# List-scheduling all engine streams of a cosine-attention + projection kernel from one dependency graph, with an early first projection

## Chip, cores, metric

The kernel runs on one core of a Trainium2 chip. The metric is the device time of one execution in microseconds (us), as the median of several. The profiled execution has its own length, called the span. Nearly all executions were in the fast state; one each of tp_late, skd_r3 and best_u3 was slow, and a few of the kernel before. The medians in the tables are over all executions; for these three the text uses those of the fast ones. Chips and calls differ by about 0.7% (the kernel before had medians from 539.53 to 543.15 us), so each run is compared with executions of the kernel before on the same chip in the same call.

## The reference, cut to what matters

```python
q_n = q / (norm(q) + 1e-6);  k_n = k / (norm(k) + 1e-6)   # 8 batches, 12 heads, 448 tokens, 64 wide
attn = softmax(q_n @ k_n.T / 0.1);  o = attn @ v
x = o.transpose(0, 2, 1, 3).reshape(3584, 768)
h = x @ w_in               # 768 x 2048: the first projection
out = (h * cos(h)) @ w_out # 2048 x 768: the second projection
```

## The kernel before

Heads are worked in pairs: 48 pairs, three to a unit, two units (six pairs) to a batch. A pair is transposed, scored, exponentiated on ACT and attended on PE, which also forms the row sums of the exponentials. Six pairs of a batch make `xT`, the input of the batch's first projection: 96 matmuls of 128x448, in eight groups each followed by a sine on ACT and a multiply on DVE. The second projection is 896 matmuls in all, 16 per half tile, and is dealt out in eights between the parts of later pairs, to fill PE while ACT works.

Each engine runs its own stream in the order in which the program adds operations. Waits come from keys: an operation waits for the last writer of what it reads, and for the last writer and all readers of what it writes.

```python
for t in reads:
    w = self.writer.get(t)
    if w is not None: dep(w, True)
for t in writes:
    w = self.writer.get(t)
    if w is not None and w is not o: dep(w, False)
    for r in self.readers.get(t, ()): dep(r, False)      # write after read
...
self.ops[eng].append(o)                                  # program order is engine order
```

The row sums lie in a layout in which a reciprocal is slow. So each unit sends them on a round trip: gathered by four DMAs to 128 partitions, inverted on DVE, written to DRAM, read back broadcast, then multiplied.

```python
def around(u, kq):
    ...
    if u >= 1:
        if kq == 2: gather(u - 1)                        # SP: sums <- xu
        if kq == 5: recip(u - 1); spread(u - 1)          # DVE; SP: scr <- rcp
        if kq == 8: broadcast(u - 1)                     # SP: RB <- scr
    if u >= 2 and kq < UP: normalise(u - 2, kq)          # DVE: xT <- xu * RB
LAG = 4
for u in range(NU):
    for p in range(UP):
        ...                                              # scores, attend, transposes, fills
        if p == 0 and u >= LAG and u % 2 == 0:
            m1((u - LAG) // 2)                           # first projection of batch 0 in unit 4
```

Because of `LAG = 4`, the first projection of batch 0 comes after 13 pairs. Until then there is nothing to fill PE with.

Of the kernel before, what the change touches and what calls it, by code (L numbers as in the profile page):

```python
# [13 lines left out]
class Op:  # L14
    __slots__ = ("eng", "fn", "pos", "waits", "inc", "count", "dma", "dcount", "known")


class Program:
# [4 lines left out]

    ENGINES = ("PE", "ACT", "DVE", "POOL", "SP")

    def __init__(self, new_sem):
        self.new_sem = new_sem
        self.ops = {e: [] for e in self.ENGINES}
        self.known = {e: {} for e in self.ENGINES}
        self.writer = {}  # L30
        self.readers = {}
        self.dma_count = {}
        self.by_dma = {}

    def op(self, eng, fn, reads=(), writes=(), dma=None):
        o = Op()
        o.eng, o.fn, o.dma, o.inc, o.count = eng, fn, dma, False, None
        o.pos = len(self.ops[eng])
        need = {}

        def dep(y, raw):
            if y.dma is not None:
                k, v = ("dma", y.dma), y.dcount
            else:
                if y.eng == eng and (dma is None and (not raw or eng == "PE")):
                    return
                k, v = ("eng", y.eng), y.pos + 1
            if k not in need or need[k][0] < v:
                need[k] = (v, y)

        for t in reads:
            w = self.writer.get(t)
            if w is not None:
                dep(w, True)
        for t in writes:
            w = self.writer.get(t)
            if w is not None and w is not o:
                dep(w, False)
            for r in self.readers.get(t, ()):
                dep(r, False)  # L60
        known = self.known[eng]
        o.waits = []
        for k, (v, y) in sorted(need.items(), key=lambda i: str(i[0])):
            if known.get(k, 0) >= v:
                continue
            o.waits.append((k, v, y))
            if y.dma is None:
                y.inc = True
        for k, v, y in o.waits:
            known[k] = max(known.get(k, 0), v)  # L70
            for kk, vv in y.known.items():
                if known.get(kk, 0) < vv:
                    known[kk] = vv
        o.known = dict(known)
        if dma is not None:
            self.dma_count[dma] = self.dma_count.get(dma, 0) + 1
            o.dcount = self.dma_count[dma]
        for t in writes:
            self.writer[t] = o
            self.readers[t] = []  # L80
        for t in reads:
            self.readers.setdefault(t, []).append(o)
        self.ops[eng].append(o)
        return o

    def final_dma(self, names):
        o = Op()
        o.eng, o.dma, o.inc, o.count, o.known = "SP", None, False, None, {}
        o.fn, o.pos = None, len(self.ops["SP"])
        o.waits = [(("dma", n), self.dma_count[n], None) for n in names]  # L90
        self.ops["SP"].append(o)

    def emit(self, nc):
        sems = {}
        for e in self.ENGINES:
            n = 0
            for o in self.ops[e]:
                if o.inc:
                    n += 1
                    o.count = n  # L100
            if n:
                sems[("eng", e)] = self.new_sem()
        for d in self.dma_count:
            sems[("dma", d)] = self.new_sem()

        def run(name, e):
            for o in self.ops[name]:
                for k, v, y in o.waits:
                    e.wait_ge(sems[k], 16 * v if k[0] == "dma" else y.count)
                if o.fn is None:  # L110
                    continue
                inst = o.fn(e)
                if o.dma is not None:
                    inst.then_inc(sems[("dma", o.dma)], 16)
                elif o.inc:
                    inst.then_inc(sems[("eng", name)], 1)
# [24 lines left out]
def bass_cosine_attention__then__act_gcu_kernel(  # L141
# [15 lines left out]
    NG = UP * NU  # L157
    NJ = 4
# [31 lines left out]
    vraw = sb("vraw", [NP, UH * NJ * D], F32)  # L190
# [9 lines left out]
    RB = sb("RB", [128, UP * S], F32)  # L200
# [5 lines left out]
    ones = sb("ones", [NP, 32], BF16)  # L206
# [19 lines left out]
    RBv = RB.ap().rearrange("p (g s) -> p g s", g=UP)  # L226
# [3 lines left out]
    PHs = [("AV", AVv), ("SC0", SCv[0]), ("SC1", SCv[1])]  # L230

    P = Program(new_sem)


    P.op("POOL", lambda e: e.iota(iot.ap(), [[1, NP]], base=0, channel_multiplier=-1), writes=["iot"])
    P.op("DVE", lambda e: e.tensor_scalar(ident.ap(), iot.ap(), 0, None, ALU.is_equal), ["iot"], ["ident"])
    P.op("DVE", lambda e: e.memset(cst.ap()[:, 0:1], math.pi / 2.0), writes=["cst"])
    P.op("DVE", lambda e: e.memset(cst.ap()[:, 1:2], 1e-12), writes=["cst"])
    P.op("POOL", lambda e: e.memset(ones.ap(), 1.0), writes=["ones"])
    P.op("ACT", lambda e: e.preload_act_table_set("natural_log_exp_and_others"))  # L240


# [4 lines left out]
    def load(u, p0, p1):  # L247
        i = u % 2
        keys = [("raw", i, p) for p in range(p0, p1)]
        h = slice(2 * p0, 2 * p1)  # L250
        for x, t in enumerate((q, k)):
            o = P.op("SP", lambda e, x=x, t=t: e.dma_start(
                rawv[i][:, h, NJ * x : NJ * x + NJ, :].rearrange("p h s d -> p h (s d)"),
                src(t, u, 2 * p0, 2 * (p1 - p0))), writes=keys if x == 0 else [], dma="raw%d_%d" % (i, p0))
        for t in keys:
            P.writer[t] = o

    def load_v(u):
        P.op("SP", lambda e: e.dma_start(vraw.ap().rearrange("p (h c) -> p h c", h=UH), src(v, u, 0, UH)),
             writes=["vraw"], dma="vraw")  # L260


    def squares(u, p, eng="POOL"):
        i = u % 2
        x = raw[i].ap()[:, p * 2 * NS * D : (p + 1) * 2 * NS * D]
        if eng == "ACT":
            P.op("ACT", lambda e: e.activation(sq[p].ap(), x, ACT.Square), [("raw", i, p)], [("sq", p)])  # L267
        else:
            P.op(eng, lambda e: e.tensor_tensor(sq[p].ap(), x, x, ALU.mult), [("raw", i, p)], [("sq", p)])  # L269

    def reduce(u, p):
        i = u % 2
        P.op("DVE", lambda e: e.tensor_reduce(out=n2[i].ap()[:, p * 2 * NS : (p + 1) * 2 * NS],  # L273
                                              in_=sq[p].ap().rearrange("p (x d) -> p x d", d=D),
                                              axis=mybir.AxisListType.X, op=ALU.add),
             [("sq", p)], [("n2", i, p)])

    def rnorm(u, p0, p1):
        i = u % 2
        w = slice(p0 * 2 * NS, p1 * 2 * NS)  # L280
        P.op("ACT", lambda e: e.activation(lnn[i].ap()[:, w], n2[i].ap()[:, w], ACT.Ln, bias=cst.ap()[0:NP, 1:2]),
             [("n2", i, p) for p in range(p0, p1)] + ["cst"], [("lnn", i, p0)])
        P.op("ACT", lambda e: e.activation(rn[i].ap()[:, w], lnn[i].ap()[:, w], ACT.Exp, scale=-0.5),  # L283
             [("lnn", i, p0)], [("rn", i, p) for p in range(p0, p1)])

    def scale(u, p, parts=(("POOL", 0, 8),)):
        i = u % 2
        h = slice(2 * p, 2 * p + 2)
        for eng, s0, s1 in parts:
            P.op(eng, lambda e, s0=s0, s1=s1: e.tensor_tensor(  # L290
                qksv[i][:, s0:s1, h, :].rearrange("p s h d -> p h s d"), rawv[i][:, h, s0:s1, :],
                bass.AP(rn[i], p * 2 * NS + s0, [[UH * NS, NP], [NS, 2], [1, s1 - s0], [0, D]]), ALU.mult),
                [("raw", i, p), ("rn", i, p)], [("qks", i, p, s) for s in range(s0, s1)])

    def vcast(u, p):
        i = u % 2
        w = slice(2 * NJ * D * p, 2 * NJ * D * (p + 1))
        P.op("POOL", lambda e: e.tensor_copy(va[i].ap()[:, w], vraw.ap()[:, w]), ["vraw"], [("va", i, p)])


    def transposes(g):
        u, p, j = g // UP, g % UP, g % 2
        i = u % 2
        for s in range(NS):
            P.op("PE", lambda e, s=s: e.transpose(TP.ap()[:, NP * s : NP * s + NP],  # L305
                                                  qksv[i][:, s, 2 * p : 2 * p + 2, :], ident.ap()),
                 [("qks", i, p, s), "ident"], ["TP"])
        P.op("DVE", lambda e: e.tensor_copy(qkT[j].ap(), TP.ap()[:, 0 : 2 * S]), ["TP"], [("qkT", j)])  # L308

    def scores(g, c):  # L310
        j, z = g % 2, c % 2
        for a in range(2):
            r = slice(64 * a, 64 * a + 64)
            P.op("PE", lambda e, r=r, a=a: e.matmul(  # L314
                SCv[z][0:NP, a, 0:S], qkT[j].ap()[r, S + NP * c : S + NP * c + NP], qkT[j].ap()[r, 0:S],
                start=True, stop=True), [("qkT", j)], ["SC%d" % z])
        P.op("ACT", lambda e: e.activation(PXv[j][:, c], SCv[z][0:NP, :, 0:S], ACT.Exp, scale=1.0 / TAU),  # L317
             ["SC%d" % z], [("PX", j, c)])

    def attend(g, eng):  # L320
        u, p, j = g // UP, g % UP, g % 2
        i = u % 2
        for c in range(NJ):
            for a in range(2):
                P.op("PE", lambda e, a=a, c=c: e.matmul(  # L325
# [268 lines left out]
```

## Time and profile before

| | before |
|---|---|
| median (range, 3 runs) | 539.53 us (539.48 to 541.54) |
| span | 538.9 us |
| PE busy | 471.6 us, 88% |
| ACT, DVE, POOL busy | 288.4, 257.7, 220.5 us |

The first fence shows stretches of the kernel before (the windows view): start and end, length, busy time of each engine with its instruction count, mean granted clock of TensorE, DMA share of its 16 engines, GB/s.

```profile
0.00:118.00 118.00, 72.71 (x444) 27.92 (x445) 51.95 (x63) 53.87 (x73) 80.89 (x73) 0.90 0.88 188
166.73:279.20 112.47, 110.19 (x803) 55.61 (x802) 63.89 (x75) 74.80 (x89) 52.94 (x37) 1.00 0.49 125
444.00:538.90 94.90, 82.10 (x456) 44.46 (x456) 29.78 (x40) 17.92 (x18) 0.00 (x0) 0.98 0.17 45
```

A cycle of two batches in the middle has PE busy for 110.2 of 112.5 us at full clock: order alone cannot gain much there. The beginning loses 45 us and the end 13.

The second fence is a part of the chain of waits of the kernel before, the work that ended last followed back: start, length, what.

```profile
83.86 8.01 DMA RB<-scr
...
96.43 7.60 DMA sums<-xu
...
106.91 5.17 DMA RB<-scr
...
112.11 0.46 DVE xT L371
...
118.02 1.11 PE AV L381 x5
```

Most of this part of the chain is the round trip: gather 7.6 us, broadcast 5 to 8. The third fence is the timeline of PE in the kernel before: start, length, instructions, and in brackets the idle time before them with its releaser.

```profile
110.08 2.43 PE L381 MATMUL AV<-xT,W 128*128 128x448 bf16 x12
112.35 4.70 PE L381 MATMUL SC<-xT,W 128*128 128x448 bf16 x24
118.02 2.43 PE L381 MATMUL AV<-xT,W 128*128 128x448 bf16 x12 [0.97 <-DVE gT L386]
```

The first projection really begins at 110.08. The entry at 118.02 in the chain is where the chain comes back to PE after a small stop inside the projection.

### The profile page before, as it was taken

To read this page: it belongs to the slowest core of one execution; us is meant where nothing else is said; L and a number is where in the kernel's file an instruction comes from. 1 tells how busy PE (TensorE), PEld (TensorE's weight loads), DVE (VectorE), ACT (ScalarE), POOL (GpSimd) and SP (SyncE) were. 2 spreads that over 40 slices of the span, in tenths; PEclk is the share of its full clock that TensorE was granted. 3 is DMA by queue.
4 is the path that set the end of the run, shared out by engine and by line. 5 is a ranking of instruction groups with operands and counts; after the bars stand their busy time and mean duration, and the time that the engine had idled before them with its cause. 6 is when DMAs were issued, how large, how long until landed. Compare 5 with 4: busy or idle time off the path is not lost.

```text
span 538.9 us, 7716 instructions
## 1 busy us (share of the span) xinstructions
PE 471.6 (88%) x3200; PEld 230.7 (43%) x3200; DVE 257.7 (48%) x311; ACT 288.4 (54%) x344; POOL 220.5 (41%) x169
## 2 busy tenths in 40 slices
PE   1477674798999999999999999999899999779896
PEld 0122221243444545455445554554455445344463
DVE  3415553554366546544755465556475324413421
ACT  2355353565777586647774777367756674202200
POOL 4796956530855085505580459018721400000000
PEclk9999976799999999999999999999999999899999
DMA  8699899680467056902781287217501331210023
GB/s 202 125 204 210 162 201 198 152 203 1 112 174 189 1 127 170 235 1 59 210 211 26 60 209 190 75 30 205 145 24 31 85 82 24 60 58 1 29 60 88
DMA packets 51490, 62.36 MB, mean 116 GB/s; under 512 B 9984, under 2 KB 44288, under 8 KB 51456
## 3 DMA queue, kind: packets, MB, share of 16 engines
q1 hardware_dynamic: 47552, 55.58, 40.7%
q0 software_dynamic: 3904, 6.29, 7.1%
q8 instruction: 25, 0.41, 0.3%
q14 instruction: 9, 0.07, 0.0%
HBM read 56.62 MB, written 11.18 MB: 126 GB/s over the span
## 4 chain that ended last, share of the span: by engine, by line
PE 64%; DMA 16%; DVE 10%; ACT 4%; SPq 3%; POOL 2%; issue 1%; DVEq 0%; ACTq 0%
PE PO L420 20%; PE SC L381 16%; PE AV L381 10%; DMA sums<-xu 6%; DMA RB<-scr 6%; PE AV L325 5%; PE SC L314 5%; PE AV L331 3%; DMA raw<-in_k_dram 3%; DVE xT L371 3%; ACT PX L317 3%; PE SC L420 2%; DVE n L273 2%; PE TP L305 2%; SPq L345 2%; DMA scr<-rcp 2%
## 5 line engine op out<-in xcount | busy, mean ns | idle before, releaser
L317 ACT ACTIVATE PX<-SC 112x896 bf16<-112x896 f32 x192 | 164.0, 915 | 85.8 <-PE SC L314 85.8
L290 POOL TENSOR_TENSOR qks<-raw,rn 112x1024 bf16<-112x1024 f32 (+1 forms) x48 | 90.5, 1884 | 193.1 <-ACT rn L283 193.0
L420 PE MATMUL PO<-W,gT 128*128 128x384 bf16 x784 | 143.1, 330 | 9.5 <-DVE osb L428 9.5
L420 PEld LDWEIGHTS PO<-W,gT 128*128 128x128 bf16 x784 | 71.5, 98 | 78.9 <-issue 18.3
L314 PE MATMUL SC<-qkT 64*112 64x448 bf16 x384 | 70.4, 428 | 32.6 <-ACT PX L317 16.7
L269 POOL TENSOR_TENSOR sq<-raw 112x1024 bf16<-112x1024 f32 x47 | 92.2, 1985 | 9.0 <-DMA raw<-in_k_dram 8.9
L381 PE MATMUL SC<-xT,W 128*128 128x448 bf16 x480 | 94.7, 352 | 0.0
L384 ACT ACTIVATE cosb<-SC,cst 128x896 f32<-128x896 f32 x40 | 40.3, 1008 | 49.9 <-PE SC L381 47.8
L371 DVE TENSOR_TENSOR xT<-xu,RB 128x448 bf16<-128x448 f32 x48 | 47.3, 995 | 38.6 <-DMA RB<-scr 38.6
L381 PEld LDWEIGHTS SC<-xT,W 128*128 128x128 bf16 x480 | 47.0, 98 | 43.8
L386 DVE TENSOR_TENSOR gT<-SC,cosb 128x896 bf16<-128x896 f32 x40 | 43.6, 1090 | 40.8 <-ACT cosb L384 40.7
L273 DVE TENSOR_REDUCE n<-sq 112x16 f32<-112x1024 bf16 x48 | 57.5, 1209 | 7.7 <-ACT sq L267 4.1
L381 PE MATMUL AV<-xT,W 128*128 128x448 bf16 x288 | 58.4, 353 | 2.1 <-ACT xu L335 1.0
L325 PE MATMUL AV<-PX,va 112*64 112x448 bf16 x384 | 54.5, 414 | 0.0
L308 DVE COPY qkT<-TP 128x896 bf16<-128x896 bf16 x48 | 29.7, 618 | 51.4 <-PE TP L305 51.4
L428 DVE COPY osb<-PO 128x384 f32<-128x384 f32 x49 | 27.0, 551 | 54.1 <-PE PO L420 53.9
L384 ACT ACTIVATE cosb<-AV,cst 128x896 f32<-128x896 f32 x24 | 24.2, 1008 | 52.8 <-PE AV L381 51.5
L314 PEld LDWEIGHTS SC<-qkT 64*112 64x112 bf16 x384 | 21.8, 136 | 66.8 <-ACT PX L317 34.7
L305 PE MATMUL TP<-ident,qks 112*128 112x112 bf16 x384 | 31.8, 235 | 18.8 <-POOL qks L290 10.8
L381 PEld LDWEIGHTS AV<-xT,W 128*128 128x128 bf16 x288 | 27.7, 98 | 29.4 <-issue 2.9
L386 DVE TENSOR_TENSOR gT<-AV,cosb 128x896 bf16<-128x896 f32 x24 | 26.1, 1089 | 29.1 <-ACT cosb L384 29.1
L305 PEld LDWEIGHTS TP<-ident,qks 112*128 112x128 bf16 x384 | 26.1, 109 | 32.7 <-POOL qks L290 14.7
(32 smaller groups left out, 230.5 us busy)
## 6 DMA issues: line engine op xcount, KB each, us to landing
vraw<-in_v_dram SPq DMA_DIRECT2D x16, 672.0 KB, 6.0
RB<-scr SPq DMA_DIRECT2D x32, 336.0 KB, 4.7
raw<-in_q_dram SPq DMA_DIRECT2D x15, 672.0 KB, 7.9
raw<-in_k_dram SPq DMA_DIRECT2D x15, 672.0 KB, 9.4
W<-in_moe_w_in_dram POOLq DMA_DIRECT2D x12, 256.0 KB, 6.5
W<-in_moe_w_out_dram POOLq DMA_DIRECT2D x8, 384.0 KB, 8.9
out_dram<-osb SPq DMA_DIRECT2D x8, 336.0 KB, 3.2
out_dram<-osb SPq DMA_DIRECT2D x8, 288.0 KB, 2.6
```

The costliest lines, as they stand in the source:

```text
L269: P.op(eng, lambda e: e.tensor_tensor(sq[p].ap(), x, x, ALU.mult), [("raw", i, p)], [("sq", p)])
L273: P.op("DVE", lambda e: e.tensor_reduce(out=n2[i].ap()[:, p * 2 * NS : (p + 1) * 2 * NS], in_=sq[p].ap().rearrange("p (x d) -> p x d", d=D ...
L290: P.op(eng, lambda e, s0=s0, s1=s1: e.tensor_tensor(qksv[i][:, s0:s1, h, :].rearrange("p s h d -> p h s d"), rawv[i][:, h, s0:s1, :], bass ...
L305: P.op("PE", lambda e, s=s: e.transpose(TP.ap()[:, NP * s : NP * s + NP], qksv[i][:, s, 2 * p : 2 * p + 2, :], ident.ap()), [("qks", i, p, ...
L314: P.op("PE", lambda e, r=r, a=a: e.matmul(SCv[z][0:NP, a, 0:S], qkT[j].ap()[r, S + NP * c : S + NP * c + NP], qkT[j].ap()[r, 0:S], start=T ...
L317: P.op("ACT", lambda e: e.activation(PXv[j][:, c], SCv[z][0:NP, :, 0:S], ACT.Exp, scale=1.0 / TAU), ["SC%d" % z], [("PX", j, c)])
L325: P.op("PE", lambda e, a=a, c=c: e.matmul(AVv[64 * a : 64 * a + 64, 0, 0:S], vav[i][:, NJ * (2 * p + a) + c, :], PXv[j][:, c, a, :], start ...
L371: P.op("DVE", lambda e: e.tensor_tensor(xTv[b % 2][:, UP * i + p, :], xuv[i][:, 0, p, :], RBv[:, p, :], ALU.mult), ["RB", ("xu", i, p)], [ ...
L381: P.op("PE", lambda e, n=n, c=c, a=a: e.matmul(ph[:, a, 0:S], W1v[:, c, 128 * n : 128 * n + 128], xTv[b % 2][:, c, :], start=(c == 0), sto ...
L384: P.op("ACT", lambda e: e.activation(cosv[cz], ph[:, :, 0:S], ACT.Sin, bias=cst.ap()[:, 0:1], scale=1.0), [name, "cst"], [("cos", cz)])
L386: P.op("DVE", lambda e: e.tensor_tensor(gTv[:, 2 * gi : 2 * gi + 2, S * (b % 2) : S * (b % 2) + S], ph[:, :, 0:S], cosv[cz], ALU.mult), [n ...
L420: P.op("PE", lambda e, po=po, f=f, col=col, hf=hf: e.matmul(po[:, 0:HW], gTv[:, f, col : col + 128], W2v[:, f, HW * hf : HW * hf + HW], st ...
```

## The change

Operations are now collected with costs and dependencies, and every engine's stream is list-scheduled from one model, `play`. The first projection of batch 0 follows pairs 0 to 5 directly; their sums are inverted on the spot (logarithm and exponential on ACT, or a reciprocal on DVE) without the round trip. Later ones come after pair 3 of the batch after next. The second projection is spread evenly over pairs, matmuls on zeros fill early gaps of PE, normalising moves to POOL, loads of units 2 and later move from SP to ACT, weights come in 4 + 4 large DMAs instead of 20, score weights are 128 wide, `RB` is doubled, and the last second projections use several PSUM banks.

```diff
+    RATE = {"SP": 220e3, "ACT": 220e3, "POOL": 220e3}          # bytes per us
+    def play(self):
+        ...
+        server = {e: 0.0 for e in self.RATE}
+            if o.dma is not None:
+                o.end = max(o.end + 1.7, o.start + 2.2)
+                if o.nbytes > self.SMALL:
+                    server[e] = max(server[e], o.start + 1.0) + o.nbytes / self.RATE[e]
+                    o.end = max(o.end, server[e] + 1.0)
... (an engine takes the ready operation with the earliest deadline; the result is a fixed stream)
+    load_v(0, [("raw", 0, 0)])
+    load_v(1, [("raw", 0, 0)])
+    for x in range(NQ):
+        load_w1(x, [("raw", 0, 1)])
...
+    DIRECT = {0: "ACT", 1: "DVE", 2: "ACT", 3: "DVE", 4: "ACT", 5: "ACT"}
...
+    for g in range(PB):
+        pair(g, 0, 0)
+    load(2, 0, UP, reads=[("W1", 1)])
+    norms(2, 0)
+    for x in range(NQ):
+        load_w2(x, [("W1", 1)])
+    load(3, 0, UP, reads=[("W2", 0)])
+    attend(PB - 1, DIRECT[PB - 1])
+    load_v(3)
+    transposes(PB)
+    m1(0)
... (pairs 6 to 47; from b = 2 on, the first projection of batch b - 1 after pair 3 of batch b)
+    attend(NG - 1, None)
+    chain(NU - 1)                                              # the round trip of the last unit
+    banks[0] = [("PO", PO.ap())] + [(n, x[:, 0, :]) for n, x in PHs[1:]]
+    m2_fill(10 ** 6)
+    m1(B - 1)
```

The `reads` of loads have no data in them. They only say "not before this has landed". So that `load_v` and `load_w1` come after the first q/k loads, they are entered as readers of `raw` buffer 0.

## The prediction

> **What bounds the kernel now.** PE is busy 471.6 of 538.9 us (88%, page). By windows: 72.7 of the first 118 us; then 110.2 of 112.5 us in each cycle of two batches, clock 1.00; the last 95 us lose 12 again. So the steady state is bound by TensorE and the loss is the beginning: up to 118 us the chain of waits is mostly the row-sum round trip (gather, reciprocal, spread, broadcast). The first of eight first projections starts at 118.0 us, after 13 of 48 head pairs; nothing else can fill TensorE before it. The granted clock is 0.60 from 75 to 100 us.
>
> **What must be done anyway (timeline, chain).** First projection: 96 matmuls in 18.16 us, 145 us in all. Second: 16 in 2.60 us, 146 us in all. Attention on TensorE: about 3.0 us a pair (scores twice 0.52 to 0.62, attend 0.88, sums 0.49, transposes 0.49), some 0.1 of each being the change of mode. That matches the Trainium skill, "TensorEngine Tiling (Array Packing)", Key Properties (changing the tiling mode drains the array): eight second-projection matmuls take 1.41 us after such a change, 1.30 without.
>
> **What changes.**
> 1. Batch 0 is projected directly behind its six pairs, whose sums are inverted on ACT or DVE without the round trip. First exponential at about 10.5 us, from 12.7. Then ACT has 24 exponentials of 0.84 us, squares, eight half-width Ln/Exp and small ones, about 30 us, so attention ends near 42. But in the instruction order 45 filler matmuls and the transposes of pair 6 stand ahead of the projection; those wait for unit 2, whose load waits for a part of W1, then 6 us of POOL squares and a scale. I expect the projection at about 49 us (44 to 55).
> 2. 42 pairs, not 35, then come behind that point: +21 us.
> 3. Fillers keep the clock up early and compute nothing.
> 4. Steady state: the same matmuls. 128-wide score weights and order save some 0.1 us a pair; normalising moves from DVE to POOL (about 0.9 us each, estimated from POOL's 1.9 us for 1024 columns). A batch cycle of 54 to 56 us, from 56.2.
> 5. Pairs 6 to 15 have little filling: ACT and PE both need about 4.3 us a pair; 4 to 6 us are lost to coupling.
> 6. End: three banks end the single-bank waits (0.6 us a half), but after the last pair 64 matmuls (10.4 us) cover a round trip of about 18 us: some 8 us idle.
>
> **Sum.** 49 + 145 + 146 + 42 x 2.97 (125) = 465; coupling 5, entries and exits of first projections 5, end 8 + 2, last store 4: 489. Allowing for some overestimates I say 485 us, range 470 to 502; faster 0.97, same 0.02, slower 0.01.
>
> **What would show it.** The first projection at 44 to 55 us, after fillers and transposes waiting for POOL; PE over 95% busy from there to the last pair; 5 to 10 us idle before the last first projection, waiting for the POOL multiply; ACT nearly full between the first and second first projection; clock near 1.00 after 10 us.
>
> **What would make it wrong.** W1, W2 and q/k loads colliding in the first 70 us (over 20 MB); the fixed order turning late DMAs into stalls on POOL, hence late transposes; four pairs of slack (about 20 us) being too short for the round trip (17.4 us from gather to broadcast in one measured case, plus copy and multiplies), a stall in each batch.

## The result and the profile after

The changed kernel took 515.55 us (514.12 to 519.57, four runs), against 540.53. The ratio is 0.9539, with an interval of 0.9478 to 0.9599. Ratios here are the mean time of one kernel's fast runs over that of the other's of the same rounds, so not quite the ratio of the medians. It is faster by 4.6%, where I had expected about 10%; 515.55 lies above the range.

The windows view of the changed kernel, columns as above:

```profile
0.00:64.10 64.10, 50.05 (x309) 21.12 (x310) 27.39 (x37) 32.50 (x51) 35.28 (x32) 0.92 1.05 206
84.03:137.27 53.24, 43.76 (x384) 18.87 (x385) 22.40 (x31) 42.89 (x56) 37.23 (x25) 0.97 0.56 122
195.93:306.39 110.46, 109.53 (x802) 53.74 (x800) 53.58 (x68) 69.18 (x83) 61.42 (x41) 1.00 0.50 115
466.55:512.30 45.75, 41.04 (x224) 22.11 (x224) 13.20 (x16) 9.34 (x9) 0.00 (x0) 0.95 0.13 35
```

The cycle of two batches is 110.46 us, 2.0 less than before, and full. The first projection begins near 64 us, not 49. The stretch up to the second one (84 to 137 us) holds 43.8 us of PE work in 53.2 us. In the first 64 us the packets of the DMA engines add up to 1.05 of the time of 16 engines, at 206 GB/s (packets overlap; skd_r3 below reaches 1.13 and 229 GB/s, so this is no ceiling).

The chain of waits of the changed kernel, in part:

```profile
8.46 17.46 DMA W<-in_moe_w_in_dram
...
35.52 17.58 DMA raw<-in_q_dram
53.09 0.07 issue
53.17 3.19 POOL sq L445 x2
...
59.54 1.91 POOL sq L445
61.45 1.86 POOL qks L468
63.31 0.05 issue
63.35 0.74 PE TP L484 x8
```

Read from below: the transposes of pair 6 stand ahead of the projection in PE's order; they wait for POOL's scale, this for POOL's squares, and these for unit 2's load, which was issued only at 35.5 us and took 17.6 us more. The PE timeline of the changed kernel around the two places where it stops longest without being at work on anything useful:

```profile
48.34 1.70 PE L526 MATMUL AV<-PX,ones 112*64 112x448 bf16 x8 [5.35 <-ACT xu L549]
...
51.47 9.60 PE L677 MATMUL PO<-zt 128*128 128x448 bf16 x45
63.35 0.74 PE L484 MATMUL TP<-ident,qks 112*128 112x112 bf16 x8 [2.28 <-POOL qks L468]
63.89 2.44 PE L601 MATMUL AV<-xT,W 128*128 128x448 bf16 x6
...
466.55 4.02 PE L601 MATMUL AV<-xT,W 128*128 128x448 bf16 x12 [5.99 <-POOL xT L578]
```

The 45 matmuls at 51.47 are the fillers on zeros; attention of batch 0 was over by then. The stop of 5.35 us before 48.34 is ACT's, whose timeline in the changed kernel is:

```profile
40.98 6.72 ACTq L422 DMA_DIRECT2D raw<-in_q_dram  x1
47.75 0.54 ACT L549 ACTIVATE xu<-AV 128x448 f32<-128x448 f32 x1 [5.97 <-issue]
```

ACT stood in the issue of the second half (q) of unit 3's load, while the inversion for batch 0 waited behind it. The order key was not what held it: W2's first quarter had landed at 37.2, and the first half (k) was issued at 40.63. The issue itself took 6.72 us, while both halves of unit 2's load, issued on the same queue, were still on their way; it ended within 0.4 us of the landing of the first of them (47.37). In sp_loads below, SP's issue of the same half takes 6.65 us. What the issue waits for is not shown. The Trainium skill ("Perfetto Trace Analysis", Tensor Engine Instruction) says that ACT, DVE and GPSIMD are strictly first in, first out; the trace agrees in that ACT did nothing else in these 6 us. The start of the projection did not pay for them: in sp_loads ACT has no such stop, and the projection begins at 63.7 all the same.

The last line of the PE fence is the end: 64 matmuls cover only a part of the last unit's round trip, and PE idles 5.99 us. Afterwards 12 matmuls take 4.02 us instead of the 2.43 that the same 12 took in the kernel before. The skill ("TensorE: Matmul & The Clock Gate", Part 1) says that an idle array falls back to half its clock and needs about 3.4 us of work to be released; the trace agrees (335 ns each on average against 203; the granted clock is 0.50 from the restart to 469.70, for 3.15 us, and 1.00 from 469.80 on).

In the stretch after the first projection, the PE stops of over 1 us in the changed kernel are:

```profile
87.41 0.52 PE L498 MATMUL SC<-qkT 64*128 64x448 bf16 x2 [2.40 <-ACT PX L503]
...
115.71 0.55 PE L498 MATMUL SC<-qkT 64*128 64x448 bf16 x4 [2.73 <-DVE qkT L490]
...
137.27 0.92 PE L601 MATMUL AV<-xT,W 128*128 128x448 bf16 x4 [3.76 <-POOL xT L578]
```

and DVE, ahead of the stop at 115.71:

```profile
107.30 0.61 DVE L490 COPY qkT<-TP 128x896 bf16<-128x896 bf16 x1
112.45 0.20 DVE L568 TENSOR_REDUCE rcp<-sums 128x21 f32<-128x42 f32 x1 [4.53 <-DMA sums<-xu]
...
114.96 0.61 DVE L490 COPY qkT<-TP 128x896 bf16<-128x896 bf16 x1
```

DVE stood before the sum of the gathered pieces, in an order planned with a gather of about 3.5 us (four issues of 0.46 and 1.7 us in the model); it took 9.6 us from the first issue (102.86). The copy that PE needed stood behind it.

### The profile page after: what moved, and what is told of

The parts are those of the page before. It is cut to its first block, busy times and chain, and to the rows that moved or that the text cites. A ratio compares the mean times of both kernels' runs of the same rounds, so it can differ in the third digit from the quotient of the medians.

```text
span 512.3 us, 7897 instructions
## 1 busy us (share of the span) xinstructions
PE 475.0 (93%) x3308; PEld 229.8 (45%) x3308; DVE 223.1 (44%) x286; ACT 283.1 (55%) x345; POOL 238.2 (47%) x164
## 3 DMA queue, kind: packets, MB, share of 16 engines
q10 hardware_dynamic: 19264, 19.27, 14.9%
## 4 chain that ended last, share of the span: by engine, by line
PE 73%; DMA 10%; issue 5%; POOL 4%; ACT 3%; DVE 2%; SPq 1%; ACTq 0%; POOLq 0%; DVEq 0%
PE PO L641 22%; PE SC L601 18%; PE AV L601 11%; PE SC L498 7%; PE AV L512 6%; DMA raw<-in_q_dram 4%; DMA W<-in_moe_w_in_dram 3%; PE AV L520 3%; PE TP L484 3%; PE SC L641 2%; ACT PX L503 2%; DMA sums<-xu 1%; POOL sq L445 1%; DMA RB<-scr 1%; POOL xT L578 1%
## 5 line engine op out<-in xcount | busy, mean ns | idle before, releaser
L503 ACT ACTIVATE PX<-SC 112x896 bf16<-112x896 f32 x192 | 165.2, 916 | 59.1 <-PE SC L498 58.3
L641 PE MATMUL PO<-W,gT 128*128 128x384 bf16 x752 | 137.6, 329 | 2.5 <-DVE osb L653 2.2
L468 POOL TENSOR_TENSOR qks<-raw,rn 112x1024 bf16<-112x1024 f32 x47 | 88.6, 1905 | 61.9 <-ACT rn L461 46.9
L641 PEld LDWEIGHTS PO<-W,gT 128*128 128x128 bf16 x752 | 67.9, 98 | 70.0 <-issue 21.4
L445 POOL TENSOR_TENSOR sq<-raw 112x1024 bf16<-112x1024 f32 x45 | 84.1, 1893 | 31.9 <-DMA raw<-in_q_dram 27.8
L578 POOL TENSOR_TENSOR xT<-xu,RB 128x448 bf16<-128x448 f32 x42 | 46.5, 1136 | 109.5 <-DMA RB<-scr 109.3
L498 PE MATMUL SC<-qkT 64*128 64x448 bf16 x384 | 58.9, 361 | 7.4 <-ACT PX L503 3.9
L592 ACT ACTIVATE cosb<-AV,cst 128x896 f32<-128x896 f32 x24 | 24.2, 1007 | 59.1 <-PE AV L601 57.9
L512 PE MATMUL AV<-PX,va 112*64 112x448 bf16 x384 | 47.4, 367 | 1.1 <-DMA va<-in_v_dram 1.1
L541 DVE COPY xu<-AV 128x896 f32<-128x896 f32 x21 | 22.9, 1091 | 31.3 <-PE AV L520 31.3
L484 PE MATMUL TP<-ident,qks 112*128 112x112 bf16 x384 | 27.5, 214 | 4.8 <-POOL qks L468 4.2
L498 PEld LDWEIGHTS SC<-qkT 64*128 64x128 bf16 x384 | 14.2, 94 | 37.9 <-issue 17.1
```

Source lines behind the costliest of these rows:

```text
L445: pool(lambda e, x=x, y=y: e.tensor_tensor(y, x, x, ALU.mult), [("raw", i, p)], keys, 0.1 + n * 1.78e-3, label="sq")
L468: f = lambda e, s0=s0, s1=s1: e.tensor_tensor(qksv[i][:, s0:s1, h, :].rearrange("p s h d -> p h s d"), rawv[i][:, h, s0:s1, :], bass.AP(rn ...
L484: r = e.transpose(TP.ap()[:, NP * s : NP * s + NP], qksv[i][:, s, 2 * p : 2 * p + 2, :], ident.ap())
L498: t = e.matmul(SCv[z][:, a, 0:S], qkT[j].ap()[r, NP * c : NP * c + 128], qkT[j].ap()[r, S : 2 * S], start=True, stop=True)
L503: act(lambda e: e.activation(PXv[j][:, c], SCv[z][0:NP, :, 0:S], ACT.Exp, scale=1.0 / TAU), ["SC%d" % z], [("PX", j, c)], 2 * S, "E", labe ...
L512: t = e.matmul(AVv[64 * a : 64 * a + 64, 0, 0:S], vav[i][:, NJ * (2 * p + a) + c, :], PXv[j][:, c, a, :], start=(c == 0), stop=(c == NJ - 1))
```

## The experiments

The theory at this point: most of the miss is the start. Unit 2's load is issued late because its order keys make it wait for too much, it is slow because W2 shares the DMA engines with it, and the streams stand in a fixed order made for other times. The rivals: the position of the transposes, W2's traffic alone, the loads on ACT's stream, or the fillers.

### First call: four single causes

```diff
 tp_late:    transposes(PB) moved from before m1(0) to before its seventh group
             (the expectation says between seventh and eighth; edit and trace have it before the seventh)
 w2_behind:  -        load_w2(x, [("W1", 1)])
             +        load_w2(x, [("raw", 0, 0)])     # again a reader of raw 0: now behind unit 2's load
 sp_loads:   -    load(2, 0, UP, reads=[("W1", 1)])
             +    load(2, 0, UP, "SP", reads=[("W1", 1)])       # load(3, ...) likewise
 no_fill:    +    P.filler = None
```

> Edit: the transposes of pair 6 are put between the seventh and the eighth part of batch 0's first projection instead of ahead of it. Theory G (the gate: the projection stood behind transposes that wait for unit 2's load): the first projection starts at about 52 us (when the last of batch 0's normalised heads is written, 51.7 us in the profile) instead of 63.9, and the time falls by 9 to 12 us, to about 504. Rival (what follows needs the same load, or the weights are not there yet): the wait only moves behind the projection, less than 4 us are won.

> Edit: the four W2 loads wait for unit 2's q and k load instead of for the second quarter of W1. Theory C (contention: unit 2's load took 17.6 us because W2 shared the DMA engines with it): it lands at about 44 us instead of 53.1, the first projection starts at about 54 and the time falls by 7 to 10 us. Rival O (the load is late because ACT issues it late and in order): it lands less than 4 us earlier, and the time falls by less than 4.

> Edit: the loads of units 2 and 3 are issued by SP, which has nothing else to do then, instead of by ACT. Theory O (ACT's order): unit 2's load is issued at about 26 us instead of 35.1 and lands 6 to 9 us earlier; ACT's stop of 6.0 us before the inverse of pair 4's sums is gone; first projection at about 56, time 6 to 8 us less. Theory C (contention): issued earlier, but the DMA engines are full in any case (share 0.99 to 1.2 up to 56 us), so it lands at most 4 us earlier and the time falls by less than 4; the ACT stop goes but nothing hangs on it.

> Edit: no filler matmuls. If they keep the clock up and are worth it: the granted clock in the first 60 us falls from about 0.92 to 0.6 or less, attention of batch 0 ends later, and the time rises by 2 to 6 us. If they are useless, because the first projection waits for unit 2's load anyway: time within 1.5 us. If they stand in the way of real work: time falls.

| run | median us | ratio to before [95%] | first projection starts at | second starts at |
|---|---|---|---|---|
| after (its own call) | 515.55 | 0.9539 [0.9478, 0.9599] | 63.9 | 137.3 |
| tp_late | 516.69 | 0.9515 [0.9414, 0.9616] | 50.2 | 125.5 |
| w2_behind | 516.51 | 0.9549 [0.9474, 0.9624] | 52.3 | 136.2 |
| sp_loads | 519.62 | 0.9627 [0.9532, 0.9722] | 63.7 | 134.6 |
| no_fill | 519.03 | 0.9595 [0.9520, 0.9670] | 63.8 | 140.5 |

None is clearly different from the changed kernel in time (all intervals overlap its own), yet two of them begin the projection 12 to 14 us earlier. So the start can be mended, and the gain is given back later. In tp_late the first projection itself stops 3.86 us (at 63.06, for DVE's multiply), and the way from the first projection to the third takes 141.3 us, in w2_behind 143.0. In three profiles of the changed kernel (this one and the repeats after_again and after_last below) it takes 131.9, 133.7 and 134.0. Its two halves are less steady: from the second to the third it is 58.5, 62.9 and 62.7 us with no edit at all, so differences of some 4 us in one half are not read as effects here. In w2_behind the load was issued at 33.7 and landed at 40.8, in 7.1 us instead of 17.6, since W2 was not on its way (nor was unit 3's load, which comes behind W2; but in keys below unit 3's load is issued after unit 2's has landed, 48.6 against 41.7, and that one still takes 16.9 us, with weights on the way). Unit 3's load then shared with W2 and took 17.6 us. PE and DVE of w2_behind, in this order (timelines):

```profile
75.55 4.64 PE L601 MATMUL SC<-xT,W 128*128 128x448 bf16 x12 [9.48 <-DVE gT L594]
```

```profile
73.18 1.22 DVE L450 TENSOR_REDUCE n<-sq 112x16 f32<-112x1024 bf16 x1 [9.43 <-POOL sq L445]
```

DVE's reduce for unit 3 waited for the late load, and the multiply for the projection stood behind it: 9.5 us lost in the middle of the projection. The wait was moved, not removed. The skill ("DMA: Bandwidth & Descriptors", Issuing engines are not separate DMA queues) says that transfers started by different engines run on the same 16 DMA engines; this pair of runs agrees, 7.1 us with no weights on their way against 17.6 with W2. The plan has a rate of 220 GB/s for *each* of three issuers.

sp_loads says that ACT's stream was not what delayed unit 2's load: SP issued it at 33.3 us, only 2 us earlier. On SP too it waited for something. The code shows for what: all four quarters of W1, and v. The waits come from the keys: `load_w1` and `load_v` are readers of `raw` 0, unit 2's load writes `raw` 0, and a writer waits for all readers. The order that was meant ("W1 after the first q/k load") became "unit 2's q/k load after all of W1". The traces agree: W1's last quarter landed at 33.48 us in the changed kernel and at 32.79 in sp_loads, and unit 2's load was issued from 35.10 (behind work of ACT) and from 32.97. The chain of waits of w2_behind shows the same step:

```profile
9.86 23.34 DMA W<-in_moe_w_in_dram
...
33.29 0.38 ACTq L422
...
33.70 7.09 DMA raw<-in_q_dram
```

no_fill shows that the fillers did not harm: without them the projection starts at the same time (63.84), at a clock of 0.77 in the stretch before, and the total is no better.

### Second call: the false wait, the plan's DMA, and the end

```diff
 keys:       a load also writes a key of its own, ("got", u, p), and load_v and load_w1 read that one
             -    load_v(0, [("raw", 0, 0)])          ->  +    load_v(0, [("got", 0, 0)])
             -        load_w1(x, [("raw", 0, 1)])     ->  +        load_w1(x, [("got", 0, 1)])
 share (used in share_keys):
             -  server[e] = max(server[e], o.start + 1.0) + o.nbytes / self.RATE[e]
             +  at = max(server[e], o.start + 1.0)
             +  n = 1 + sum(server[x] > at for x in server if x != e)
             +  server[e] = at + n * o.nbytes / self.RATE[e]
 direct_end: DIRECT also {45: "ACT", 46: "ACT", 47: "ACT"};  attend(NG - 1, "ACT");  no chain(NU - 1)
 share_keys_tp_d: share + keys + direct_end + tp_late
```

`share` does not change what the kernel does, only what the planner believes, and with it the order of the streams.

> Edit: the loads that only want an order (W1 and v behind the first q and k) read an ordering key of their own instead of the raw buffer's key. Theory F (a false wait: as readers of the raw buffer's key, all four W1 loads and both v loads had to land before unit 2 could be loaded into that buffer): unit 2's load is issued at about 25 us instead of 33 to 36 us, lands at 40 to 44 instead of 53, and batch 0's first projection starts at 51 to 54 instead of 64. Whether the total gains it depends on the second theory, P (the fixed order was planned with three issuing queues of 220 GB/s each, while all share one set of DMA engines): then ACT and DVE will stand behind steps of unit 3, whose load lands later than planned, and part of the gain comes back as a stop inside the first projection, so total 3 to 8 us less. Without P: 10 us less.

> Edit: as keys, and the plan divides a load's rate by the number of queues that are busy when it is issued. Theory P: the order now fits the late loads; first projection at 50 to 54 us with no stop over 2 us inside it, and the span is shorter than that of keys by 3 us or more, about 500. Rival (the bytes themselves are late, order does not matter): same as keys within 2 us.

> Edit: the last three pairs invert their sums on ACT in full width, as the first six do, instead of the round trip. The idle of 6.0 us and the half-clock start (12 matmuls in 4.0 us instead of 2.27) before the last first projection go; 1.1 us of sums matmuls come in. Theory E (the end lost its time to the uncovered round trip): the span from the start of the seventh first projection to the end falls by 5 to 8 us. Rival (TensorE's work is what ends last): under 2 us.

> Edit: share_keys, tp_late and direct_end together. If the start and the end are separate losses, the gains add up: first projection at 45 to 50 us, seventh to end 5 to 8 us shorter, 492 to 500 us in all. If the stretch of pairs 6 to 15 takes up what the start gains (loads of unit 3 and W2 still have to come), the second first projection starts at 125 us or later and the total stays at 503 or more.

| run | median us | ratio to before [95%] | first projection | second | last |
|---|---|---|---|---|---|
| keys | 512.34 | 0.9467 [0.9385, 0.9549] | 57.8 | 130.8 | |
| share_keys | 502.94 | 0.9297 [0.9216, 0.9378] | 52.0 | 124.4 | 453.6 |
| direct_end | 508.92 | 0.9385 [0.9321, 0.9449] | 64.0 | | 460.2 |
| share_keys_tp_d | 499.34 | 0.9212 [0.9152, 0.9271] | 49.4 | 126.9 | |

keys and share_keys have three executions each. With the keys alone, the load was issued at 24.8 instead of 35.5, which shows the false wait. But it still took 16.9 us, with the end of W1 and W2 under way, the projection began at 57.8 and not at 51 to 54 as expected, and DVE had the norms of unit 2 planned ahead of the reciprocals of batch 0. DVE in keys (timeline):

```profile
33.65 0.62 DVE L490 COPY qkT<-TP 128x896 bf16<-128x896 bf16 x1 [0.17 <-PE TP L484]
43.66 1.22 DVE L450 TENSOR_REDUCE n<-sq 112x16 f32<-112x1024 bf16 x1 [9.39 <-POOL sq L445]
44.80 0.85 DVE L556 RECIPROCAL RB<-AV 128x112 f32<-128x112 f32 x1
```

Again an operation of the future stood in front of one of the present. Once the planner knows that loads share the DMA engines (share_keys), the order fits, and the whole start is 12 us shorter, of which little is given back (the third projection begins at 182.7 us; 195.8 to 198.2 in the three profiles of the changed kernel).

direct_end inverts the last unit's sums on the spot too. From the seventh first projection to the end of the run it took 88.6 us instead of 95.6. The stop before the last projection is gone, and with it the half clock; the PE timeline of direct_end there:

```profile
460.22 2.43 PE L601 MATMUL AV<-xT,W 128*128 128x448 bf16 x12
```

share_keys_tp_d begins the first projection earliest of all, at 49.4, but needs 139.4 us to the third, where share_keys needs 130.7: moving the transposes gives its gain back here, too.

### Third call: is it the keys, the plan, or both?

```diff
 after_again:  no edit
 share:        the edit of share alone
 skd:          share + keys + direct_end
 skd_r3:       skd, and   -    load(3, 0, UP, reads=[("W2", 0)])
                          +    load(3, 0, UP, reads=[("W1", 3)])
```

> Edit: none, the changed kernel again, on the chip and in the rounds of the next three, so that they can be compared with it and not only with the kernel before. 513 to 518 us.

> Edit: only the plan's rate is divided by the number of busy queues; the false wait on all W1 loads stays. Theory P alone (the order): the load of unit 2 is still issued at 33 to 36 us and lands at about 53, so the first projection still starts at 62 to 64 us, and nothing is won there; after it, fewer stops: under 4 us in all. If it gains 8 us or more, the order and not the false wait made the start late.

> Edit: share_keys and direct_end together. The gains of start (12.6 us in the profile of share_keys) and end (7.0 us in that of direct_end) add up: span 491 to 494 us, time 493 to 497. If they don't add up, 499 or more.

> Edit: as skd, and unit 3's load waits for the last quarter of W1 instead of the first of W2. If the stretch of pairs 6 to 15 is limited by unit 3's late load, the second first projection starts 2 to 4 us earlier than in skd. If by ACT and the round trip, no change (1 us).

| run | median us | ratio to before [95%] | first projection | second | third | last |
|---|---|---|---|---|---|---|
| after_again | 517.55 | 0.9537 [0.9499, 0.9575] | 63.6 | 134.4 | 197.3 | 468.2 |
| share | 518.60 | 0.9557 [0.9514, 0.9600] | 65.9 | 139.4 | 199.6 | |
| skd | 496.83 | 0.9163 [0.9122, 0.9203] | 53.9 | 124.8 | 184.7 | 450.4 |
| skd_r3 | 494.18 | 0.9116 [0.9069, 0.9163] | 52.1 | 122.2 | 180.9 | 446.9 |

A better plan alone wins nothing (518.60 against 517.55, inside each other's intervals): unit 2's load is then issued at 38.9 us, no earlier than before. The keys alone won about 0.7 points in their call (0.9467, against 0.9539 and 0.9537 for the changed kernel in others, which the intervals do not separate); both together won 2.4 points (share_keys, 0.9297). So neither is the cause by itself. The wait and the order planned around it were one mistake. skd shows that the gains of start and end add up (493 to 497 us expected, 496.83 measured).

skd_r3 is the best kernel: 493.23 us by its fast executions, 24 us less than the changed kernel of the same call. It differs from skd by what holds unit 3's load (W1's last quarter in place of W2's first); the intervals of the two overlap. Its windows view, for the start and the end:

```profile
0.00:52.10 52.10, 44.41 (x294) 18.83 (x295) 26.04 (x36) 32.22 (x51) 34.53 (x32) 0.97 1.13 229
446.90:491.00 44.10, 39.47 (x226) 21.66 (x223) 13.75 (x17) 9.34 (x9) 0.00 (x0) 0.98 0.16 45
```

and a part of its chain of waits:

```profile
23.36 17.23 DMA raw<-in_q_dram
...
40.67 1.90 POOL sq L447
...
43.73 0.62 DVE xT L560
...
45.34 6.52 PE PO L679 x25
51.86 0.40 PE TP L486 x8
52.26 2.27 PE AV L603 x12
```

The load still takes 17 us, but begins at 23. It is still in the chain: a multiply of DVE for batch 0 stands behind a reduce for unit 2, which waits for the load and POOL's square (PE stops 3.01 us for that multiply). Then PE is held in its own stream, by 25 fillers and the transposes. The transposes also need POOL's scale, which ended near 50.1, so the fillers keep them back by 1.6 us at most.

### Fourth call: the stretch up to the second projection

In the changed kernel this stretch lost 9.5 us (7.1 in each of the two repeats), of which 3.76 (2.3 in the repeats) waiting for POOL's normalising of unit 3. Theory: taking unit 3 (pairs 9 to 11) off the round trip, too, saves that wait. Rival: the stops come from the order of DVE's stream, and the extra ACT work (a logarithm and an exponential a pair) costs as much. The call also asks once more what the fillers are worth.

```diff
 u3_only:        DIRECT also {9: "ACT", 10: "ACT", 11: "ACT"}
 best_u3:        skd_r3 + u3_only
 best_u3_nofill: best_u3 + P.filler = None
 after_last:     no edit
```

> Edit: the changed kernel, with the sums of unit 3 (the last three pairs of batch 1) inverted on ACT at full width instead of over the round trip; nothing else. Theory R (the stretch of pairs 6 to 15 is long by the round trip: DVE stands behind the gather, 1.7 to 2.7 us, and the second first projection waits 2.3 to 3.8 us for the POOL multiply): both waits go, and the stretch falls from 50.8 to 53.3 us to 46 to 48, 1 us of it given back in sums matmuls. Theory A (ACT and PE in lockstep, as predicted): ACT gets more work, the stretch stays at 50 or more.

> Edit: skd_r3 with the same direct inverse for unit 3. Theory R: second first projection at 117 to 119 us instead of 122.2, time 2 to 5 us under that of skd_r3 (494.2), about 490. Theory A: no change or slower.

> Edit: best_u3 without filler matmuls. Now that the first projection does not wait for unit 2's late load, the clock of the first 50 us should count: if fillers earn what they are for, 2 to 5 us slower than best_u3 and a lower granted clock; if the start is bound by loads and ACT, within 1.5 us of it.

> Edit: none, the changed kernel beside these three. 513 to 518 us.

| run | median us | ratio to before [95%] | first projection | second | third |
|---|---|---|---|---|---|
| u3_only | 521.01 | 0.9590 [0.9537, 0.9644] | 63.9 | 138.4 | 200.2 |
| best_u3 | 504.46 | 0.9266 [0.9215, 0.9318] | 50.8 | 124.0 | 189.4 |
| best_u3_nofill | 508.60 | 0.9348 [0.9305, 0.9392] | 54.9 | 129.8 | 195.7 |
| after_last | 518.51 | 0.9528 [0.9480, 0.9576] | 64.2 | 135.5 | 198.2 |

The theory fell. The wait for POOL was gone in u3_only, and PE stopped elsewhere: 3.92 and 1.75 us, behind DVE, which stood 6.81 us for unit 2's gather. best_u3 is 10 us worse than skd_r3. Fillers do seem to earn something here: without them the projection begins 4.1 us later, and the run is 0.9% longer (0.9348 against 0.9266, the intervals just overlapping). The granted clock up to the projection is 0.91 instead of 1.00, unit 2's load is issued 2.6 us later and lands 3.3 us later, and the transposes wait 4.54 us for POOL's scale. So the load still sets the start; how a lower clock makes its issue late was not separated.

### Fifth call: is it the gather's time in the plan?

Theory: the loss in best_u3 was order and not work; a plan that expects a gather to last 7.8 us from its first issue (instead of 3.5) does not put DVE's sum where it must wait. Then best_u3 should gain much, and skd_r3, which was good already, should stay as it was.

```diff
 g_u3, g_skd (from best_u3, from skd_r3), in the plan alone:
 -   o.end = max(o.end + 1.7, o.start + 2.2)
 +   o.end = max(o.end + (6.0 if "gather" in o.label and o.start < 160 else 1.7), o.start + 2.2)
```

> Edit: best_u3, and the plan takes a gather of the sums before 160 us to last 7.8 us from its first issue (measured 7.5 to 9.6 in that stretch) instead of 3.5. Theory H (head of line: DVE's stream is fixed with the sum of the gathered rows too early, and everything behind it waits for the DMA): the stop of 3.4 us (scores waiting for DVE's copy) before the second first projection and the 4.2 us after it go; second first projection at 118 to 121 us, third 59 to 61 us later, time 490 to 496 instead of 504.5. If it stays at 502 or more, the loss of best_u3 is work that the direct inverse adds, not order.

> Edit: the same longer gathers in the plan of skd_r3. Theory H: its smaller stops for DVE's copy (1.1 and 0.9 us) go, the wait for the POOL multiply (2.3 us) stays or grows, as the round trip gets no shorter; time within 3 us of skd_r3's 494.2.

| run | median us | ratio to before [95%] | first projection | second | third |
|---|---|---|---|---|---|
| g_u3 | 496.07 | 0.9188 [0.9142, 0.9234] | 52.4 | 120.4 | 182.3 |
| g_skd | 506.80 | 0.9365 [0.9316, 0.9413] | 52.5 | 124.7 | 193.6 |

g_u3 came out nearly as the theory says (third projection 61.9 us after the second, 59 to 61 expected; 496.07 us, 490 to 496 expected), with the same work on every engine as best_u3 (busy times differ by at most 1.1 us): 7.6 us less by the medians of fast executions, 0.8 points by the ratios (the two ran in different calls, and their intervals just overlap). Its third projection begins 7.0 us earlier. DVE no longer waits for a gather on the way to the second projection, and its next sum, which waited 5.73 us in best_u3, does not wait either; one wait of 3.45 us remains just before the third. PE of best_u3 (timeline):

```profile
97.97 0.93 PE L500 MATMUL SC<-qkT 64*128 64x448 bf16 x4 [3.42 <-DVE qkT L492]
```

DVE of best_u3, which released it late (timeline), and then DVE of g_u3 at the same operation:

```profile
96.83 0.20 DVE L570 TENSOR_REDUCE rcp<-sums 128x21 f32<-128x42 f32 x1 [6.31 <-DMA sums<-xu]
```

```profile
98.48 0.20 DVE L570 TENSOR_REDUCE rcp<-sums 128x21 f32<-128x42 f32 x1
```

g_skd was a miss: expected within 3 us of skd_r3's 494.2, it took 506.8 (13.6 us more than the fast executions of skd_r3, in another call). From its second to its third projection it needs 68.9 us, where skd_r3 needs 58.7. PE of g_skd (timeline, two of its stops), then POOL of g_skd:

```profile
151.91 2.74 PE L643 MATMUL PO<-W,gT 128*128 128x384 bf16 x8 [2.06 <-DVE osb L655]
...
193.55 0.73 PE L603 MATMUL AV<-xT,W 128*128 128x448 bf16 x3 [3.61 <-POOL xT L580]
```

```profile
143.12 1.89 POOL L447 TENSOR_TENSOR sq<-raw 112x1024 bf16<-112x1024 f32 x1 [6.87 <-DMA raw<-in_q_dram]
```

Here POOL stood for the load of a later unit, and behind it in its stream stood three normalising multiplies of the present one, from 144.97 on; DVE's next reduce waited 4.40 us for these squares, in front of two multiplies of the projection. A truer number for one DMA gave a worse order at another place. Which of g_skd's stops costs how much of the 13.6 us was not separated, and no order was found that is good everywhere.

## Why the prediction was wrong

The prediction was right that it would be faster, and wrong in size: it said 485 us, 470 to 502, and it was 515.55. Its sum was 489, the span of the profiled run 512.3: 23 us apart.

| term | predicted | measured | difference, us |
|---|---|---|---|
| start of the first projection | 49 (44 to 55) | 63.9 | +14.9 |
| PE's idle time in pairs 6 to 15 | 5 | 53.24 - 43.76 = 9.5 | +4.5 |
| everything else | 435 | 438.9 (512.3 - 63.9 - 9.5) | +3.9 |

The first row is the same in the repeats (63.6 and 64.2 us). The split between the other two is not: there pairs 6 to 15 lose 7.1 us in each run, and the way from the second to the third projection is some 4 us longer.

- **The step that failed is the first term, "I expect the projection at about 49 us".** The chain of causes that it named was right: the fillers and the transposes of pair 6 stand ahead of the projection, those wait for POOL, POOL waits for unit 2's load. tp_late, which takes the transposes out of the way, begins the projection at 50.2 us, so some 14 of the 14.9 us are this wait for the load. (That run had only attention to wait for, which "ends near 42" in the prediction and ended at 51.5 in the changed kernel; the first exponential began at 12.98, not 10.5.) The load was mis-sized twice. "Waits for a part of W1" should have been all of W1 and v, because order keys entered as reads became write-after-read waits; that was readable in the code, and issue came at 35.5 us. And it took 17.6 us and not the 7.9 or 9.4 us that the page of the kernel before has as medians of such loads, with W2 on its way at the same time: 7.1 us without it (w2_behind). keys, share and share_keys show that removing the false wait pays in full only with an order planned for shared DMA engines: the start falls to 52 us and the ratio by 2.4 points.
- The prediction named this collision ("W1, W2 and q/k loads colliding in the first 70 us") and the fixed order ("turning late DMAs into stalls on POOL, hence late transposes") under what would make it wrong, but gave them no time in the sum, and the allowance made was of the opposite sign ("allowing for some overestimates": 489 to 485).
- "Pairs 6 to 15 ... 4 to 6 us are lost to coupling" was right that ACT and PE are close (42.9 and 43.8 us of work for ten pairs, so 4.3 to 4.4 a pair), and wrong in kind. ACT was busy for 81% of that stretch, not "nearly full". PE stopped for DVE and POOL, which stood behind round trips in their own fixed order, and 2.40 us for the first exponential after the switch of tables. That order and not work is the cost is what best_u3 against g_u3 points to (7.6 us by the medians of fast executions, intervals just overlapping); what the best order is stays open.
- "A batch cycle of 54 to 56 us" was right: 110.46 / 2 = 55.2. "PE over 95% busy from there to the last pair" held from the third first projection to the seventh (219.06 of 220.92 us), just failed in the repeats on the way from the second to the third (59.1 of 62.9 us, 94%), and failed clearly in pairs 6 to 15 (82%).
- "POOL about 0.9 us each" for normalising was too little: 1.136 us, three of which stand in front of the last first projection. The page of the changed kernel has it (part 5, groups):

```profile
L578 POOL TENSOR_TENSOR xT<-xu,RB 128x448 bf16<-128x448 f32 x42 | 46.5, 1136 | 109.5 <-DMA RB<-scr 109.3
```

- "Some 8 us idle" at the end was right in kind: 5.99 us, and about 1.6 more by the half clock after it (4.02 - 2.43). direct_end took 7.0 us off that part.
- "Clock near 1.00 after 10 us" was nearly right: 0.92 for the first 64 us (0.77 without fillers), 1.00 in the cycles. The fillers harmed nothing there.
- The miss is no accident: run again, the changed kernel took 0.9537 and 0.9528 of the time before.

## What to carry to other kernels

An edge put into a dependency graph only for order must have a key of its own: entered as a read of a buffer, it holds the buffer's next writer, too. A list schedule that becomes fixed streams on first-in-first-out engines is as good as its DMA times; share the DMA engines in the model, look in the trace for operations of a later unit that stand before those of the present one, and expect that one better number can spoil the order at another place. When an early gain does not reach the end, compare the start times of a repeated stage in both traces: they show between which two stages it was given back.

## What the Trainium skill lacked or had wrong

- "DMA: Bandwidth & Descriptors", Issuing engines are not separate DMA queues, is right but gives no size. A unit's load (k and q, 672 KB each) landed 7.1 us after the issue of its second half with no weights on their way, and after 16.4 to 19.2 us in all other runs of the changed kernel and its variants, with weight loads of another engine under way; in the changed kernel the DMA engines had a share of 1.05 and moved 206 GB/s in the first 64 us.
- The same page, Anatomy of one DMA, fits one transfer of the GpSimd path with about 2.0 us and the bytes over 436 GB/s. No page has a figure for a gather of runs of 84 bytes issued by SP: four of 5.2 KB took 9.6 us from the first issue to DVE's start here (102.86 to 112.45), and the last of them 7.60 us in the kernel before.
- "ScalarE: Activation LUTs", What ACT_TABLE_LOAD costs, has about 1283 ns for the load and some 1380 ns of drain, 2.66 us for a switch. Here, with the load placed by the program, the load took 1.28 us, but the next exponential began 1.31 us after the last sine ended (85.13 to 86.44): no drain of that length is in the trace.
- "TensorE: Matmul & The Clock Gate", Part 1, has the fall to half clock after an idle window of about 3.4 us. Here six matmuls at 63.89 ran at 407 ns each (granted clock 0.50) after a stop of only 2.28 us and eight transposes, 2.8 us together, where the fillers ahead of the stop had taken 213 ns.
- "GPSIMD Engine Reference", 3.1, gives a two-input operation at one size only (4497 ns for 2048 fp32). Scaling in proportion misleads for small ones: here 1.136 us for 448 columns and 1.89 us for 1024, both fp32 in and bf16 out, so some 0.55 us of the small one is fixed (an estimate from these two).
